# Batch 0's v read on SyncE's queue, and the block sums of v of the later batches on GpSimd, in an attention kernel with an FFN behind it

## The chip, the cores and the metric

The kernel runs on one core of a Trainium2 chip. The metric is the device time of one execution in microseconds (us); a kernel is run several times, and its median counts. A profiled execution also has a span: the time from the first to the last instruction that the trace holds.

## What is computed

Four batches, eight heads, 768 positions, 64 numbers per head. Each query sees its neighbours within 15 positions, and beside them one summary key and value for every block of 32 positions: the maximum of the block's keys and the mean of its values. The result goes through an FFN with a gate that is cut at 0 and 6.

```python
k_sum = k.reshape(B, H, nb, block, D).max(axis=3)
v_sum = v.reshape(B, H, nb, block, D).mean(axis=3)
mask_l = np.abs(pos[:, None] - pos[None, :]) < window        # window = 16
scores_s = scale * einsum(q, k_sum) + log(block)             # block = 32
a = softmax(concat([where(mask_l, scores_l, -1e9), scores_s]))
x = a @ concat([v, v_sum])          # heads side by side: 3072 x 512
h = x @ w_in                        # 512 x 2048
out = (h * clip(h + 3, 0, 6) / 6) @ w_out
```

Inputs and output are f32; the kernel multiplies in bf16.

## The kernel before, in words

The heads are taken in four pairs (p = 0 to 3; two pairs make a group g), each batch in two halves of 384 queries. A pair's keys lie in kbd and its values in vbd, both block diagonal in 128 rows: the first head in rows 0 to 63, the second in 64 to 127, zeros elsewhere. For each batch and pair:

- K (L277) transposes k on PE into a PSUM tile tp, copies it into kbd (one half by ACT, one by DVE, L302) and takes the block maxima (red, L306, and kst, L313).
- Tq (L319) transposes q in the same way; ACT writes qT (L333). In batch 0 the queries come in two parts, up to 480 and from 480 on.
- Sl (L336) makes the scores of the near keys (PE L341), ACT their exp (L344), DVE multiplies by the mask (L345). Ss (L347) makes those of the blocks (PE L351, exp on ACT L354).
- AV (L368) accumulates num (the block sums in vst first, L377, then vbd, L379) and den, ACT makes 1/den with a logarithm and an exp (lg, L395 and L396), and DVE writes x (L397).

The FFN of a half is F1 (L402; 16 steps ft, each four matmuls L409, ACT's r L412 and DVE's g L413) and F2 (L415; 48 matmuls L422, copied out by ACT L426 and stored through SyncE's queue).

Values come in three ways. For batch 0, load_vf (L123) reads v as f32 into vf, two transfers of 64 x 12 x 64 per pair. vcast (L244) copies it into vbd, one half by ACT and one by DVE. vsum0 (L251) sums it on PE with an f32 matmul (vps, L256): for each group ACT and DVE copy the sums out (L261), SyncE's queue moves them into 96 rows (vs, L263), and to_vst (L228) multiplies them by the head masks hm4 into vst. For batches 1 to 3, load_v (L115) reads v into vbd, cast to bf16 by the transfer, and load_vrows (L132) reads it once more into vr, 96 rows of 4 x 512 f32, one per block; vsum (L233) sums a row on DVE with six additions (L235, L236, L237, and three of L240), and to_vst follows with two products (L230).

What sets the order: until `start.__exit__` (L474), PE, ACT and DVE run in the order in which the code is written, and GpSimd does so in the whole program. v_first (L442) is vcast, zeroing of vbd for pairs 0 and 1, and vsum0; it is written for pair 0 and pair 1 ahead of K(0, 0), for pairs 2 and 3 near S_first(0). After L474 a table `plan` lists for each slot (one step ft of the FFN's work list L532, 16 slots per entry) which pieces of attention are issued there, and a scheduler may move them by some steps; `attention` (L489) fills it.

All loads are issued by GpSimd (POOL), one after another, and wait on POOL for their buffers. Each also waits for the load eight places ahead of it. Before the FFN the order is v of pairs 0 and 1, k and q of pair 0, v of pair 2, the mask, v of pair 3, k and q of pair 1, of pairs 2 and 3 together, hm4, then w_in in four chunks (one ahead of the others, L214), the second part of q, and w_out in four. `hold_loads` (L517) is a copy on POOL that reads a column of g of F1(0, 11), so that the loads of batch 1 are issued only after it. In batches 1 to 3, load_vrows(b + 1, g) stands in POOL's order right after vsum(b, g), and shares two buffers with it.

Of the kernel before, what the change touches and what calls it, by code (L numbers as in the profile page):

```python
# [32 lines left out]
def kernel(  # L33
# [50 lines left out]
    def load_k(b, p, n=1):  # L84

        if b < NLONG:
            t = ld.tile([RP, 2 * n, RUN, D], BF16, tag=f"kb{n}", name="kb", bufs=2)
            nc.gpsimd.dma_start(out=t[:], in_=k[b, 2 * p:2 * p + 2 * n].rearrange("h (p s) d -> p h s d", s=RUN))
        else:
            t = ld.tile([128, NT, 2, D], BF16, tag="kb", name="kb")  # L90
            load_natural(t, k, b, p)
        for i in range(n):
            kb_t[b, p + i] = t, i
# [29 lines left out]
    def load_vf(p):  # L123

        if not vf:
            t = gp.tile([128, NP, NK, D], F32, tag="g", name="vf")
            vf.update({i: t[:, i] for i in range(NP)})
        for j in range(2):
            nc.gpsimd.dma_start(out=vf[p][64 * j:64 * j + 64],  # L129
                                in_=v[0, 2 * p + j].rearrange("(n k) d -> k n d", k=KB))  # L130

    def load_vrows(b, g):  # L132
# [9 lines left out]
    def load_w_in(c):  # L142
        w = d_ff // 4
        nc.gpsimd.dma_start(out=w_in_sb[:, :, c * w:(c + 1) * w], in_=w_in_v[:, :, c * w:(c + 1) * w])

    def load_w_out(c):
# [4 lines left out]
    ctx.enter_context(tc.manual_schedule(engines={ET.Pool}))  # L151
    start = tc.manual_schedule(engines={ET.PE, ET.Activation, ET.DVE})
    start.__enter__()
    load_vf(0)
    ident = const.tile([128, 128], BF16, tag="id", name="ident")
    nc.gpsimd.memset(ident[:], 1.0)
    nc.gpsimd.affine_select(out=ident[:], in_=ident[:], compare_op=ALU.is_equal, fill=0.0, base=0,
                            channel_multiplier=1, pattern=[[-1, 128]])
    load_vf(1)
    load_k(0, 0)  # L160
    load_q(0, 0, 1, 0)
    load_vf(2)


    mask = const.tile([128, WIN], BF16, tag="mask", name="mask")
    nc.gpsimd.memset(mask[:], 1.0)
    for j in range(2):
# [2 lines left out]
                                channel_multiplier=-1, pattern=[[1, WIN]])  # L170
        nc.gpsimd.affine_select(out=m, in_=m, compare_op=ALU.is_ge, fill=0.0, base=2 * HALO,
                                channel_multiplier=1, pattern=[[-1, WIN]])
    load_vf(3)
    load_k(0, 1)
    load_q(0, 1, 1, 0)
    load_k(0, 2, 2)
    load_q(0, 2, 2, 0)


    hm4 = const.tile([RS, 4, D], F32, tag="hm4", name="hm4")  # L180
# [27 lines left out]
            nc.vector.memset(ind[32 * i:32 * i + 32, par, par, i:i + 1], 1.0)  # L208
    for p in range(NP):
        zero_off_diagonal(nc.vector if p < 2 else nc.scalar, kbd[p][:])  # L210
    for p in range(2, NP):
        zero_off_diagonal(nc.vector, vbd[p])
    NK0 = 7
    load_w_in(0)  # L214

    def zero_rest():
        for p in range(NP):
# [7 lines left out]
        nc.vector.memset(half_c[:], 0.5)  # L225


    def to_vst(g, a):  # L228
        for par in range(2):
            nc.vector.tensor_tensor(vst[2 * g + par][:], a.unsqueeze(1).to_broadcast([RS, 2, D]), hmv[par],  # L230
                                    op=ALU.mult)

    def vsum(b, g):  # L233
        r, w = vr_t[b, g], BLK // PCS * D
        nc.vector.tensor_tensor(r[:, 0:1, 0:w], r[:, 0:1, 0:w], r[:, 2:3, 0:w], op=ALU.add)  # L235
        nc.vector.tensor_tensor(r[:, 1:2, 0:w], r[:, 1:2, 0:w], r[:, 3:4, 0:w], op=ALU.add)  # L236
        nc.vector.tensor_tensor(r[:, 0, 0:w], r[:, 0, 0:w], r[:, 1, 0:w], op=ALU.add)  # L237
        while w > D:
            w //= 2
            nc.vector.tensor_tensor(r[:, 0, 0:w], r[:, 0, 0:w], r[:, 0, w:2 * w], op=ALU.add)  # L240
        to_vst(g, r[:, 0, 0:D])


    def vcast(p):  # L244
# [32 lines left out]
    def K(b, p):  # L277

        red = work.tile([128, NB], BF16, tag="red", name="red")
        if b >= NPE:  # L280
            t = kT[b, p]
            for j in range(2):
                rows = slice(64 * j, 64 * j + 64)
                nc.vector.tensor_copy(kbd[p][rows, :, rows], t[rows].rearrange("p (n c) -> p n c", c=KB))
            nc.vector.reduce_max(red[:], t[:].rearrange("p (n c) -> p n c", c=BLK), axis=AX.X)
        else:
            pool, tag = (ps_o, "o") if b == 0 else (ps_s, "s")
            tp = pool.tile([128, S], BF16, tag=tag, name="tp")
            (t, i), long = kb_t[b, p], b < NLONG
            if long:  # L290
                for s in range(RUN):
                    for j in range(2):
                        nc.tensor.transpose(tp[64 * j:64 * j + 64, s * RP:(s + 1) * RP], t[:, 2 * i + j, s], ident[0:RP, 0:RP])
            else:
                for s in range(NT):
                    nc.tensor.transpose(tp[:, s * 128:(s + 1) * 128], t[:, s].rearrange("p h d -> p (h d)"), ident[:])
            for j in range(2):
                copy = nc.scalar.copy if j == 0 or (b == 1 and p % 2 == 1) else nc.vector.tensor_copy
                rows = slice(64 * j, 64 * j + 64)
                o = kbd[p][rows, :, rows]  # L300
                if long:
                    copy(o.rearrange("p n (c s) -> p n c s", s=RUN), tp[rows].rearrange("p (s n c) -> p n c s", s=RUN, n=NK))  # L302
                else:
                    copy(o, tp[rows].rearrange("p (n c) -> p n c", c=KB))
            if long:
                nc.vector.tensor_reduce(red[:], tp[:].rearrange("p (s n c) -> p n s c", s=RUN, n=NB), axis=AX.XY, op=ALU.max)  # L306
            else:
                nc.vector.reduce_max(red[:], tp[:].rearrange("p (n c) -> p n c", c=BLK), axis=AX.X)
        off = 2 * NB * (p % 2)
        o = kst[p][:, off:off + 2 * NB].rearrange("p (h n) -> p h n", h=2)  # L310
        if b == 0:
            for i in range(2):
                nc.vector.tensor_tensor(  # L313
                    o[:, :, i * NK:(i + 1) * NK], red[:].rearrange("p (n i) -> p i n", i=2)[:, i:i + 1].to_broadcast([128, 2, NK]),
                    hmk[:, :, 0:NK], op=ALU.mult)
        else:
            nc.vector.tensor_tensor(o, red[:].unsqueeze(1).to_broadcast([128, 2, NB]), hmk[:], op=ALU.mult)
# [50 lines left out]
    def AV(b, p, half):  # L368
# [1 line left out]
        if s not in xt:  # L370
            xt[s] = xp.tile([128, NP, HALF], BF16, tag="x", name="x")
        a, asm = at[p], asum[b, p // 2, half]
        alt = b == 0 and (p == 3 or p == 1 and half == 1)
        pool = ps_o if alt else ps_n
        num = pool.tile([128, HALF], F32, tag="o" if alt else "num", name="num")
        bl = blocks_of(half)
# [51 lines left out]
            nc.sync.dma_start(out=out[row:row + 128], in_=o[:])  # L428


    load_w_in(1)
    load_q(0, 0, 4, 1)
    for c in range(2, 4):
# [6 lines left out]
            Sl(0, p, lo, hi)  # L440

    def v_first(p):  # L442
        vcast(p)
        if p < 2:
            zero_off_diagonal(nc.scalar, vbd[p])
        vsum0(p)

    v_first(0)
    zero_rest()
    v_first(1)  # L450
    K(0, 0)
    Tq(0, 0, 0)
    v_first(2)
    S_first(0)
    v_first(3)
    K(0, 1)
    Tq(0, 1, 0)
    S_first(1)
    nc.vector.tensor_scalar_mul(osum4[:], hm4[:], float(BLK))
    to_vst(0, vs96[0][:])  # L460
    K(0, 2)
    Tq(0, 2, 0)
    Ss(0, 0, 0)
    AV(0, 0, 0)
    K(0, 3)
    Tq(0, 3, 0)
    S_first(2)
    AV(0, 1, 0)
    to_vst(1, vs96[1][:])
    S_first(3)  # L470
    Ss(0, 1, 0)
    AV(0, 2, 0)
    AV(0, 3, 0)
# [5 lines left out]
    def at_slot(s, f):  # L479
        plan.setdefault(int(s), []).append((s, f))  # L480
# [5 lines left out]
            at_slot(2 * p + 3, lambda g=p // 2: Ss(0, g, 1))  # L486
        at_slot(12 + p, lambda p=p: AV(0, p, 1))

    def attention(b, t_slot, t_gap, av_slot, av_gap, loads):  # L489
        for p in range(NP):  # L490
            s = t_slot + t_gap * p
            if b < NPE:
                at_slot(s + 1, lambda p=p: Tq(b, p))
            else:
                at_slot(s - 3, lambda p=p: X(b, p))
            at_slot(s, lambda p=p: K(b, p))
            s += 4
            at_slot(s, lambda p=p: Sl(b, p, 0, 4))
            at_slot(s + 0.5, lambda p=p: Sl(b, p, 4, 8))
            at_slot(s + 1, lambda p=p: Sl(b, p, 8, 12))  # L500
            if p % 2 == 1:
                at_slot(s + 2, lambda g=p // 2: Ss(b, g, 0))
                at_slot(s + 3, lambda g=p // 2: Ss(b, g, 1))
                at_slot(s, lambda g=p // 2: vsum(b, g))
                if b + 1 < B:
                    at_slot(s, lambda g=p // 2: load_vrows(b + 1, g))
            if 2 <= b + 1 < B:
                at_slot(s + 1, lambda p=p: (load_k(b + 1, p), load_q(b + 1, p)))
        for i, (p, half) in enumerate(((0, 0), (1, 0), (2, 0), (3, 0), (0, 1), (1, 1), (2, 1), (3, 1))):
            at_slot(av_slot(i), lambda p=p, half=half: AV(b, p, half))  # L510
            if half == 1 and b + 1 < B:
                if p % 2 == 1:
                    at_slot(av_slot(i), lambda g=p // 2: load_v(b + 1, g))

    pace = const.tile([1, 2], BF16, tag="pace", name="pace")

    def hold_loads(t, ft):  # L517

        nc.gpsimd.tensor_copy(pace[:], gt[t][0:1, ft, 0:2])

    at_slot(11, lambda: hold_loads(0, 11))
    for g in range(2):
        at_slot(11.5, lambda g=g: (load_k(1, 2 * g, 2), load_q(1, 2 * g, 2)))
        at_slot(15, lambda g=g: load_v(1, g))
        at_slot(15, lambda g=g: load_vrows(1, g))
    attention(1, 28, 3, lambda i: (41, 42, 45, 46, 50, 52, 54, 56)[i], 2, None)
    for b in range(2, B):
        base = 48 + 32 * (b - 2)
        order = (14, 16, 24, 26, 18, 20, 28, 30)
        attention(b, base, 5, lambda i, base=base: base + order[i], 2, None)  # L530

    work_list = ([(0, None), (1, 0), (None, 1), (2, None)] + [(t, t - 1) for t in range(3, NTILE)]  # L532
                 + [(None, NTILE - 1)])
# [40 lines left out]
```

## Time and profile before

| | |
|---|---|
| median of 6 runs | 262.68 us (260.35 to 263.92) |
| the profiled execution: time, span | 261.92 us, 260.2 us |
| PE busy | 239.8 us (92%) |
| DVE busy | 157.0 us (60%) |
| ACT busy | 167.7 us (64%) |
| POOL busy | 71.7 us (28%), 104 instructions |
| POOL's queue of transfers | 19.14 MB in 53264 packets |
| SyncE's queue of transfers | 6.34 MB in 3664 packets |
| vf loads (L129, POOL) | 8 of 192 KB, 3.9 us from issue to landing |
| vr loads (L136, POOL) | 6 of 768 KB, 7.8 us |

A group line of the profile names the code line, engine, operation, what it writes and reads, and how often; then busy time and the mean of one. In brackets stands how long the engine was idle before it and who ended that. PEld is PE's weight load, SP is SyncE, and a q behind an engine is its sequencer, which issues transfers. A PE that counts as busy is not PE at its full rate: matmuls overlap, and their ends are modelled. In a line of the timeline the first number is the start, the second the time until the last of the merged instructions ended.

### The profile page before, as it was taken

What the parts mean: (1) busy time and instruction counts of PE and PEld (TensorE: products, weight loads), DVE (VectorE), ACT (ScalarE), POOL (GpSimd) and SP (SyncE); (2) the same over time, 40 slices, a digit from 0 to 9 for tenths busy, and PEclk for the clock granted to TensorE, in tenths of its full rate; (3) what the DMA queues carried; (4) which work ended last, traced back from release to release, by engine and by line L of the source; (5) the groups of instructions that cost most, each with busy time, mean ns of one, the idle gap of its engine ahead of it and who ended that gap; (6) DMA issues with size and microseconds to landing.
All of it is one profiled execution on the core that took longest, in us unless ns stands there. A gap on an engine that the chain in (4) does not pass through costs nothing.

```text
span 260.2 us, 4992 instructions
## 1 busy us (share of the span) xinstructions
PE 239.8 (92%) x1936; PEld 135.8 (52%) x1936; DVE 157.0 (60%) x362; ACT 167.7 (64%) x325; POOL 71.7 (28%) x104
## 2 busy tenths in 40 slices
PE   0957889999999979999999999999999999999993
PEld 0225546644455546666645555566655555555541
DVE  6396656624899667998894477657544444444400
ACT  7565679833787858998666656766856655555410
POOL 8993000847281402796710400000000000000000
PEclk9996899999999999999999999999999999999999
DMA  3999995699999912999991551101011111101122
GB/s 111 181 151 199 206 207 91 93 190 230 219 241 98 184 45 49 87 162 154 195 108 40 35 69 42 43 1 43 0 40 43 40 40 43 40 2 42 41 81 81
DMA packets 56951, 25.80 MB, mean 99 GB/s; under 512 B 45152, under 2 KB 52320, under 8 KB 56928
## 3 DMA queue, kind: packets, MB, share of 16 engines
q0 software_dynamic: 53264, 19.14, 64.4%
q1 hardware_dynamic: 3664, 6.34, 6.5%
q8 instruction: 15, 0.25, 0.4%
q14 instruction: 8, 0.07, 0.1%
HBM read 31.98 MB, written 6.29 MB: 147 GB/s over the span
## 4 chain that ended last, share of the span: by engine, by line
PE 60%; DMA 15%; DVE 11%; POOL 7%; ACT 4%; issue 3%; POOLq 0%; ACTq 0%
PE hp L409 24%; PE op L422 23%; DMA vr<-in_v_dram 10%; DVE g L413 3%; DMA qb<-in_q_dram 3%; PE num L379 2%; POOL vf L129 2%; POOL vbd L120 2%; DMA kb<-in_k_dram 2%; PE num L377 2%; PE den L383 2%; PE den L386 2%; PE sl L341 2%; PE ss L351 1%; ACT r L412 1%
## 5 line engine op out<-in xcount | busy, mean ns | idle before, releaser
L409 PE MATMUL hp<-x,win 128*128 128x384 bf16 x512 | 104.5, 326 | 2.8 <-DVE g L413 1.5
L412 ACT ACTIVATE r<-hp,half_c 128x384 f32<-128x384 f32 x128 | 73.5, 580 | 45.6 <-PE hp L409 44.8
L422 PE MATMUL op<-wout,g 128*128 128x512 bf16 x384 | 101.0, 379 | 0.0
L413 DVE SCALAR_TENSOR_TENSOR g<-r,hp 128x384 bf16<-128x384 f32 x128 | 69.8, 552 | 46.1 <-ACT r L412 46.0
L409 PEld LDWEIGHTS <-win 128*128 128x128 bf16 x512 | 47.4, 98 | 36.9 <-issue 6.0
L422 PEld LDWEIGHTS <-g 128*128 128x128 bf16 x384 | 36.6, 98 | 32.5 <-issue 0.6
L397 DVE TENSOR_TENSOR x<-num,lg 128x384 bf16<-128x384 f32 x32 | 17.8, 555 | 25.1 <-ACT lg L396 23.8
L120 POOL DMA_DIRECT2D vbd<-in_v_dram x24 | 18.1, 776 | 36.5 <-PE num L379 33.3
L395 ACT ACTIVATE lg<-den 128x384 f32<-128x384 f32 x32 | 15.7, 491 | 17.8 <-PE den L390 9.2
L344 ACT ACTIVATE at<-sl 128x376 bf16<-128x376 f32 (+2 forms) x48 | 22.3, 486 | 3.7 <-PE sl L341 3.6
L426 ACT COPY ot<-op 128x512 f32<-128x512 f32 x24 | 13.8, 583 | 8.9 <-PE op L422 8.8
L345 DVE TENSOR_TENSOR at<-at,mask 128x376 bf16<-128x376 bf16 (+2 forms) x48 | 16.2, 350 | 3.6 <-ACT at L344 3.5
L396 ACT ACTIVATE lg<-lg 128x384 f32<-128x384 f32 x32 | 16.8, 525 | 0.8
L379 PEld LDWEIGHTS <-vbd 128*128 128x128 bf16 x224 | 13.2, 101 | 7.9 <-issue 4.5
L341 PE MATMUL sl<-qT,kbd 128*128 128x94 bf16 x192 | 14.6, 209 | 2.2 <-DVE kbd L302 2.1
L341 PEld LDWEIGHTS <-kbd 128*128 128x128 bf16 x192 | 12.0, 99 | 8.9 <-DVE kbd L302 3.0
L113 POOL DMA_DIRECT2D qb<-in_q_dram x16 | 13.5, 865 | 4.7 <-DMA vr<-in_v_dram 2.7
L379 PE MATMUL num<-at,vbd 128*128 128x94 bf16 (+2 forms) x224 | 14.4, 204 | 0.0
L256 PE MATMUL vps<-vf,ind 128*8 128x384 f32 x16 | 8.2, 662 | 6.4 <-DMA vf<-in_v_dram 6.4
L113 POOL DMA_DIRECT2D kb<-in_k_dram x16 | 13.5, 866 | 0.0
L377 PE MATMUL num<-asum,vst 96*128 96x384 bf16 x32 | 10.8, 337 | 2.3 <-DVE x L397 1.5
L386 PE MATMUL den<-at,obd 128*128 128x384 bf16 x32 | 11.1, 345 | 0.0
(82 smaller groups left out, 218.3 us busy)
## 6 DMA issues: line engine op xcount, KB each, us to landing
out_dram<-ot SPq DMA_DIRECT2D x24, 256.0 KB, 2.1
vr<-in_v_dram POOLq DMA_DIRECT2D x6, 768.0 KB, 7.8
vbd<-in_v_dram POOLq DMA_DIRECT2D x24, 96.0 KB, 4.2
win<-in_moe_w_in_dram POOLq DMA_DIRECT2D x4, 512.0 KB, 12.0
wout<-in_moe_w_out_dram POOLq DMA_DIRECT2D x4, 512.0 KB, 18.9
vf<-in_v_dram POOLq DMA_DIRECT2D x8, 192.0 KB, 3.9
kb<-in_k_dram POOLq DMA_DIRECT2D x16, 96.0 KB, 6.8
qb<-in_q_dram POOLq DMA_DIRECT2D x16, 96.0 KB, 6.4
```

Source lines behind the costliest of these rows:

```text
L113: nc.gpsimd.dma_start(out=t[:, :, j], in_=src[b, 2 * p + j].rearrange("(s p) d -> p s d", p=128))
L120: nc.gpsimd.dma_start(out=vall[rows, p, lo:hi, rows], in_=v[b, 2 * p + j].rearrange("(n k) d -> k n d", k=KB)[:, lo:hi])
L341: nc.tensor.matmul(sp[:, i * WIN:(i + 1) * WIN], kbd[p][:, t], qT[p][:, PAD - HALO + t * KB:PAD - HALO + t * KB + WIN], start=True, stop=True)
L344: nc.scalar.activation(a, sp[:, 0:n * WIN].rearrange("p (n c) -> p n c", c=WIN), AF.Exp, scale=scl)
L379: nc.tensor.matmul(num[:, lo:hi], vbd[p][:, t], a[:, t, off:off + hi - lo], start=False, stop=(i == len(bl) - 1))
L386: nc.tensor.matmul(d3, ones, a[:, t0:t1, HALO:HALO + KB], start=False, stop=False)
L396: nc.scalar.activation(lg[:], lg[:], AF.Exp, scale=-1.0)
L397: nc.vector.tensor_tensor(xt[s][:, p], num[:], lg[:], op=ALU.mult)
L409: nc.tensor.matmul(hp[:], w_in_sb[:, kt, ft * 128:(ft + 1) * 128], xt[t][:, kt], start=(kt == 0), stop=(kt == NP - 1))
L412: nc.scalar.activation(r[:], hp[:], AF.Relu, bias=half_c[:], scale=1.0 / 6.0)
L413: nc.vector.scalar_tensor_tensor(gt[t][:, ft], r[:], 1.0, hp[:], op0=ALU.min, op1=ALU.mult)
L422: nc.tensor.matmul(op[:], gt[t][:, ft, ts * 128:(ts + 1) * 128], w_out_sb[:, ft], start=(ft == 0), stop=(ft == NFT - 1))
```

## The change

Three things. First, load_vf issues on SyncE, and all eight of its transfers come first; on POOL k and q of all pairs now come before the mask and hm4. Second, the first chunk of w_in is held by a copy on POOL that reads a column of vf of pair 3, so it is issued when that has landed. Third, the six additions and two products of vsum run on GpSimd, and the slots of vsum and load_vrows are set anew.

With it go edits of the order in batch 0: vsum0 comes ahead of vcast; v_first(p) stands after Tq(0, 0), S_first(0), K(0, 2) and Ss(0, 0, 0); vbd is zeroed for pairs 0 and 1 on ACT at the start and for pairs 2 and 3 on DVE after v_first(0); AV(0, 0, 0) comes after S_first(2). K's tp of batch 0 is taken from ps_h, where Tq's is, and num and den of batch 0 come from ps_o for more pairs.

```diff
         for j in range(2):
-            nc.gpsimd.dma_start(out=vf[p][64 * j:64 * j + 64],
+            nc.sync.dma_start(out=vf[p][64 * j:64 * j + 64],
...
-    load_vf(0)
+    for p in range(NP):
+        load_vf(p)
+    load_k(0, 0)
+    load_q(0, 0, 1, 0)
     ident = const.tile([128, 128], BF16, tag="id", name="ident")
...
-    load_vf(1)
-    load_k(0, 0)
-    load_q(0, 0, 1, 0)
-    load_vf(2)
+    load_k(0, 1)
+    load_q(0, 1, 1, 0)
+    load_k(0, 2, 2)
+    load_q(0, 2, 2, 0)
...
+    pace = const.tile([128, 2], F32, tag="pace", name="pace")
+    def hold_loads(src):
+        nc.gpsimd.tensor_copy(pace[0:src.shape[0], 0:1], src)
...
-    for p in range(2, NP):
-        zero_off_diagonal(nc.vector, vbd[p])
+    for p in range(2):
+        zero_off_diagonal(nc.scalar, vbd[p])
     NK0 = 7
-    load_w_in(0)
...
-    def to_vst(g, a):
+    def to_vst(eng, g, a):
...
-        nc.vector.tensor_tensor(r[:, 0:1, 0:w], r[:, 0:1, 0:w], r[:, 2:3, 0:w], op=ALU.add)
+        nc.gpsimd.tensor_tensor(r[:, 0:1, 0:w], r[:, 0:1, 0:w], r[:, 2:3, 0:w], op=ALU.add)
...
-        to_vst(g, r[:, 0, 0:D])
+        to_vst(nc.gpsimd, g, r[:, 0, 0:D])
...
-            pool, tag = (ps_o, "o") if b == 0 else (ps_s, "s")
+            pool, tag = (ps_h, "h") if b == 0 else (ps_s, "s")
...
-        alt = b == 0 and (p == 3 or p == 1 and half == 1)
+        alt = b == 0 and (half == 0 and p != 2 or half == 1 and p % 2 == 1)
...
+    hold_loads(vf[NP - 1][:, 0, 0:1])
+    load_w_in(0)
     load_w_in(1)
...
     def v_first(p):
+        vsum0(p)
         vcast(p)
-        if p < 2:
-            zero_off_diagonal(nc.scalar, vbd[p])
-        vsum0(p)
-    v_first(0)
     zero_rest()
-    v_first(1)
     K(0, 0)
     Tq(0, 0, 0)
-    v_first(2)
+    v_first(0)
+    for p in range(2, NP):
+        zero_off_diagonal(nc.vector, vbd[p])
     S_first(0)
-    v_first(3)
+    v_first(1)
     K(0, 1)
...
     K(0, 2)
+    v_first(2)
     Tq(0, 2, 0)
     Ss(0, 0, 0)
-    AV(0, 0, 0)
+    v_first(3)
     K(0, 3)
     Tq(0, 3, 0)
     S_first(2)
+    AV(0, 0, 0)
+    S_first(3)
+    to_vst(nc.vector, 1, vs96[1][:])
     AV(0, 1, 0)
...
-                at_slot(s, lambda g=p // 2: vsum(b, g))
-                if b + 1 < B:
-                    at_slot(s, lambda g=p // 2: load_vrows(b + 1, g))
...
+        for g in range(2):
+            at_slot(sums[g], lambda g=g: vsum(b, g))
+            if b + 1 < B:
+                at_slot(rows, lambda g=g: load_vrows(b + 1, g))
...
-    attention(1, 28, 3, lambda i: (41, 42, 45, 46, 50, 52, 54, 56)[i], 2, None)
+    attention(1, 28, 3, lambda i: (41, 42, 45, 46, 50, 52, 54, 56)[i], (30, 31), 45)
...
-        attention(b, base, 5, lambda i, base=base: base + order[i], 2, None)
+        attention(b, base, 5, lambda i, base=base: base + order[i], (base + 4.5, base + 8.5) if b == 2 else (base - 11.5, base - 1.5), base + 12)
```

In POOL's order the two sums of batch 1 now stand between the loads of vr of batch 1 and the k and q loads of batch 2. Each sum of batches 2 and 3 stands right after the vbd loads of its group; the vr loads of a batch stand behind k and q loads.

More of the change, by code (lines that the diff above doesn't have):

```diff
@@ L172 @@
                                 channel_multiplier=1, pattern=[[-1, WIN]])
[L173 to L177, printed above, removed]
+    pace = const.tile([128, 2], F32, tag="pace", name="pace")
+    def hold_loads(src):
+        nc.gpsimd.tensor_copy(pace[0:src.shape[0], 0:1], src)
     hm4 = const.tile([RS, 4, D], F32, tag="hm4", name="hm4")
@@ L225, in zero_rest @@
         nc.vector.memset(half_c[:], 0.5)
-    def to_vst(g, a):
+    def to_vst(eng, g, a):
         for par in range(2):
-            nc.vector.tensor_tensor(vst[2 * g + par][:], a.unsqueeze(1).to_broadcast([RS, 2, D]), hmv[par],
+            eng.tensor_tensor(vst[2 * g + par][:], a.unsqueeze(1).to_broadcast([RS, 2, D]), hmv[par],
                                     op=ALU.mult)
@@ L234, in vsum @@
         r, w = vr_t[b, g], BLK // PCS * D
-        nc.vector.tensor_tensor(r[:, 0:1, 0:w], r[:, 0:1, 0:w], r[:, 2:3, 0:w], op=ALU.add)
-        nc.vector.tensor_tensor(r[:, 1:2, 0:w], r[:, 1:2, 0:w], r[:, 3:4, 0:w], op=ALU.add)
-        nc.vector.tensor_tensor(r[:, 0, 0:w], r[:, 0, 0:w], r[:, 1, 0:w], op=ALU.add)
+        nc.gpsimd.tensor_tensor(r[:, 0:1, 0:w], r[:, 0:1, 0:w], r[:, 2:3, 0:w], op=ALU.add)
+        nc.gpsimd.tensor_tensor(r[:, 1:2, 0:w], r[:, 1:2, 0:w], r[:, 3:4, 0:w], op=ALU.add)
+        nc.gpsimd.tensor_tensor(r[:, 0, 0:w], r[:, 0, 0:w], r[:, 1, 0:w], op=ALU.add)
         while w > D:
             w //= 2
-            nc.vector.tensor_tensor(r[:, 0, 0:w], r[:, 0, 0:w], r[:, 0, w:2 * w], op=ALU.add)
-        to_vst(g, r[:, 0, 0:D])
+            nc.gpsimd.tensor_tensor(r[:, 0, 0:w], r[:, 0, 0:w], r[:, 0, w:2 * w], op=ALU.add)
+        to_vst(nc.gpsimd, g, r[:, 0, 0:D])
     def vcast(p):
@@ L459 @@
     nc.vector.tensor_scalar_mul(osum4[:], hm4[:], float(BLK))
-    to_vst(0, vs96[0][:])
+    to_vst(nc.vector, 0, vs96[0][:])
     K(0, 2)
+    v_first(2)
     Tq(0, 2, 0)
     Ss(0, 0, 0)
-    AV(0, 0, 0)
+    v_first(3)
     K(0, 3)
@@ L467 @@
     S_first(2)
+    AV(0, 0, 0)
+    S_first(3)
+    to_vst(nc.vector, 1, vs96[1][:])
     AV(0, 1, 0)
-    to_vst(1, vs96[1][:])
-    S_first(3)
     Ss(0, 1, 0)
@@ L487, with attention @@
         at_slot(12 + p, lambda p=p: AV(0, p, 1))
-    def attention(b, t_slot, t_gap, av_slot, av_gap, loads):
+    def attention(b, t_slot, t_gap, av_slot, sums, rows):
         for p in range(NP):
@@ L513, in attention @@
                     at_slot(av_slot(i), lambda g=p // 2: load_v(b + 1, g))
[L515 to L521, printed above, removed]
+    at_slot(11, lambda: hold_loads(gt[0][0:1, 11, 0:1]))
     for g in range(2):
```

## The prediction

> **What bounds the kernel now.** I read the busy time by stage first, then the first 36 us in order of time, then the waits and the instructions around the longest PE gap in the middle. Columns of the stage view: stretch, its length, then busy time and number of instructions of PE, PEld, DVE, ACT, POOL, the granted clock, the DMA share and GB/s.
>
> ```profile
> 0.00:35.00 35.00, 22.71 (x236) 11.62 (x237) 22.53 (x76) 22.08 (x42) 20.44 (x37) 0.90 0.98 173
> 35.00:55.00 20.00, 19.67 (x208) 11.84 (x206) 12.08 (x24) 16.22 (x35) 7.29 (x11) 1.00 0.81 131
> 55.00:137.00 82.00, 78.36 (x707) 45.87 (x706) 64.82 (x149) 59.88 (x118) 41.02 (x52) 1.00 1.43 148
> 137.00:260.00 123.00, 119.06 (x793) 66.48 (x790) 57.57 (x114) 69.57 (x132) 3.00 (x4) 1.00 0.15 40
> ```
>
> From 137 us on PE is full, and nothing that the change touches is there: no gain. Until 35 us no engine is full: PE is busy 22.7 of 35. From 55 to 137 PE is nearly full, DVE at 79%. Gaps between the starts of successive matmuls, less the matmul's own columns at full clock, sum to 7.9 us between 50 and 140 us, and under 1 us after it.
>
> The start, in order of time:
>
> ```profile
> 9.69 1.50 POOL L129 DMA_DIRECT2D vf<-in_v_dram  x2
> 11.17 0.66 POOL L88 DMA_DIRECT2D kb<-in_k_dram  x1
> ...
> 12.05 6.61 SPq L263 DMA_DIRECT2D vs<-vs  x2
> ...
> 14.58 1.45 PE L256 MATMUL vps<-vf,ind 128*8 128x384 f32 x4 [0.31 <-DMA vf<-in_v_dram]
> ...
> 19.92 0.53 PE L293 MATMUL tp<-ident,kb 96*64 96x96 bf16 x16 [0.53 <-DMA kb<-in_k_dram]
> ...
> 21.25 0.44 PE L332 MATMUL tp<-ident,qb 60*64 60x60 bf16 x16 [0.80 <-DMA qb<-in_q_dram]
> ```
>
> POOL issues one load after another at 0.66 to 0.8 us each, v ahead of k and q, so the last k and q of batch 0 arrive at 19.9 and 21.2 us. x of the first half is complete at 34.5 us (the matmuls of L409 that read it start at 34.55), and the steady FFN begins there.
>
> The middle:
>
> ```profile
> DVE vr L235 <- DMA vr<-in_v_dram: 5.1, 4, 2.2
> ```
> ```profile
> 90.14 0.69 DVE L235 TENSOR_TENSOR vr<-vr 96x512 f32<-96x512 f32 x1 [2.18 <-DMA vr<-in_v_dram]
> ...
> 90.27 0.54 ACT L396 ACTIVATE lg<-lg 128x384 f32<-128x384 f32 x1
> ...
> 92.75 0.55 DVE L397 TENSOR_TENSOR x<-num,lg 128x384 bf16<-128x384 f32 x1
> ...
> 93.34 0.32 PE L377 MATMUL num<-asum,vst 96*128 96x384 bf16 x1 [1.52 <-DVE x L397]
> ```
>
> DVE stands still for vr's transfer, then does its sums ahead of L397. lg was ready at 90.8, x came at 92.75: the longest PE gap of the middle.
>
> **What the Trainium skill says.** "DMA: Bandwidth & Descriptors", Queues, rings and completion order: each DMA engine takes turns between queues, packet by packet. The trace agrees in part: SyncE's 256-byte vs packets went out at one per 90 ns and engine (first transfer) and 240 ns (second) while GpSimd's queue was full. "SBUF — State Buffer", Who interferes with whom: a DVE instruction with two SBUF inputs and a GpSimd instruction that reads SBUF lock each other out. No run here shows it yet. "TensorE: Matmul & The Clock Gate", What's actually happening: PE runs at half clock until it has been busy for some 3.4 us. Here f32 matmuls of 384 columns took 0.66 us before 11.5 us and 0.365 after it, and the records show half clock again from 21.7 to 28.6 us.
>
> **The change at the start.** Removed from POOL ahead of k and q: eight vf issues of 0.794 us. POOL now starts k(0,0) at 1.33 and, with 0.67 us per issue and 0.65 for ident between, ends its six k and q issues at about 6. A first k took 4.1 us to land, so k(0,0) is in at about 5.4 (its transposes: 11.31 before), q(0,0) at 6.2. The six transfers are 78 packets of 1024 B per DMA engine; at 90 ns each with SyncE's turns between, the last lands at about 11 (before: 21.2).
>
> Added on SP: eight issues. SP has nothing else ahead of them; queued behind them are the two vs transfers, first due at about 14. An issue there took 0.33 us (out) to 0.83 (vs); at 0.8, all are out by 7.5. The unknown is how fast 6144 packets of 256 B, 384 per DMA engine, drain. Nearest rows: 256-byte packets of SyncE's queue took 18 to 31 ns each (SBUF to SBUF), casts of 256 read bytes 32. Lower bound 17 ns, upper bound 120; below nothing is excluded, bytes must move. I take 20 to 25: 75 packets go before GpSimd's queue fills at 3.7, 31 to 78 while it is full, the rest after 11. So pair 0's v (96 packets) is in at 6 to 11, pair 1's (192) at about 13, pair 3's at about 17 (before 14.5). v is later, k and q earlier.
>
> PE's order now puts pair 0's vps before Sl(0), pair 1's vps before K(0,1), so the start hangs on pair 1's v. From 13: two cold vps matmuls 1.3; ACT vs copy 0.47, vcast 0.83, kbd copy 0.79, to about 15.9 after its queue; then DVE's list. kbd 0.96, red 0.96, kst 0.28, masks 0.6, osum 0.43, vst 0.48 = 3.7; kbd, red, kst of pair 2, 2.2; vcast, vs, vcast 1.75; pair 3's kbd, red, kst 2.2; masks, x, masks, vst 2.25; three more x 1.7: sum 13.8, to 29.7, plus 0.8 for turns in which ACT is behind: x complete at 30.5 instead of 34.5, **4.0 us** gained.
>
> Edits at nothing: vbd's zeroing on DVE (1.87 us) and ACT lies before pair 1's v is in; gone that cover, up to 1.9. K's tp in ps_h waits for the previous red, which ends about when PE gets there (0.2). num and den in ps_o are as serial as in ps_n. The mask is made by 8, needed at 11. The hold: w_in(0) goes out at about 17.5 (15.1 before), into an empty queue; 512 KB per chunk at the 200 GB/s of the DMA row is 2.6 us, so the chunks land at about 22, 25, 28 and 31, with q's second part between, and F1 needs them at 30.5 and every 2.8 us after that (4 of 0.7). Each us that v is later than 25 costs one there. wout (4 more) is in by 42, F2 starts at 46. The vs transfer of pairs 2 and 3 now meets w_in: 5.5 us as its second did before (17.96 to 23.4); out at 22, vst at 28, as in the list.
>
> **The change in the middle.** The view of the instructions that touch vr (durations are least, median, most):
>
> ```profile
> L240 DVE TENSOR_TENSOR vr<-vr x18: 214/282/421, 68.3 to 135.6; 96x256 f32<-96x256 f32 x6, 96x128 f32<-96x128 f32 x6, 96x64 f32<-96x64 f32 x6
> L230 DVE TENSOR_TENSOR vst<-vr,hm x12: 279/282/288, 69.3 to 147.7; 96x128 bf16<-96x128 f32 x12
> ...
> L235 DVE TENSOR_TENSOR vr<-vr x6: 680/687/689, 63.5 to 130.4; 96x512 f32<-96x512 f32 x6
> ```
>
> Removed from DVE, six times: 3 of 0.68 (L235 to L237), then 0.41, 0.28, 0.21 (L240), and two of 0.28 (L230) = 3.5 us, 21 in all, and 5.1 us of waiting for vr. What PE gets back, gap by gap: 93.35 (1.68) ends with x, which could have come 1.9 earlier: 1.6. 123.7 (0.80), behind L235 at 120.99 and kbd: 0.7. 133.7 and 135.4 (0.94), between vr sums: 0.8. 65.3, 68.3, 73.6 (0.96): 0.7. The many small ones: 0.4. Sum 4.2.
>
> Added on POOL, six times the same. POOL's trace has no such operation; the skill's "GPSIMD Engine Reference", Elementwise — side-by-side cycle accounting, gives 4497 ns for 2048 f32, 2.2 ns per element: 512 are 1.1 us, 1.2 with 0.1 of its own. Three of 1.2, then 0.66, 0.38, 0.24, two of 0.38: 5.6 us per sum, 34 in all. Lower bound DVE's 3.5, upper twice 5.6. Behind them in POOL's queue stand the k and q loads of the next batch. vr(1,0) lands at about 59.5 (63.5 less 4), vr(1,1) at 64: the sums run to 71. Then 16 loads of 0.82, 13.1: 71 to 84; k(2,0) is in by 75, needed at 93 (L296, near 97 before); pair 3's in by 88, needed at 108. Batch 2's sums wait for AV(1,1,1), near 98 now, and four vbd issues of 0.76: 102 to 108, vst needed at about 113 (118.6 before). Slack 5 us; at 11 us per sum it is gone. Later sums have more. Against it stand DVE's masks (0.35 us, 12 per batch, two SBUF inputs): if half a dozen per batch meet a 1.2-us sum for 0.6, DVE loses 3.6 of the 7 it gained, PE some 0.7. Net **3.5 us**. DVE at 53% instead of 79% can hide that.
>
> **The sum.** Span 260.2 less 4.0 less 3.5 = 252.7; around it 1.72 (261.92 for that execution), so 254.4. The median of the runs is 0.76 over that execution: 255.2.
>
> **Rivals.** *v too slow to help*: at 35 to 40 ns per packet pair 1's v comes at 15, pair 3's at 22; from pair 3's vps to the end are 11.2 us (vps 1.3, then 9.9 as from K(0,3), 24.65, to 34.55), so x at 33 to 34: only the middle gains, 259. For it: SyncE's 240 ns per packet beside a full queue. Against: the 18 ns. *The sums on POOL give nothing*: the port lock, or sums of 11 us that make vst late; then 258.7. For it: POOL is in order, and a late sum holds every load behind it; against: the slack above. *Slower*: SyncE's queue drains v at 80 ns per packet or more. Pair 3's v is in at 3 + 384 x 0.08 = 33.7, x at 45, 10.5 later than before, less 3.5: 269.7. It decides from 62 ns on: v at 26.8 plus 11.2 is 38, which eats the 3.5. For it: one transfer of 96 pieces took SP 0.83 us to issue, and if that grows with the pieces (768), the last issue ends near 50. Against: 128 pieces took 0.33. *Better than thought*: v at 17 ns, pair 1's at 9: 251.
>
> **How the numbers follow.** Likeliest 0.52 (its own range 252 to 258.5); v no help 0.18; sums no help 0.10; slower 0.13; better 0.07. The range 250.5 to 262.5 leaves out the slower case and half of the better one. Within 1% (260.05 to 265.3, about what this measurement can tell from no change) lie the weak ends of the second and third, 0.14; slower 0.13; faster 0.73.
>
> **What would show it.** Right: first L293 near 5.5; K(0,1) right after pair 1's vps near 13 to 15; last x of the first half near 30.5; POOL sums of 5 to 6 us; no PE gap before L377 near 90. Wrong: long waits of vps for vf, w_in after 25, vst waited for by L377, masks of over 1 us.

## The result and the profile after

The changed kernel takes 265.12 us (median of 29 runs, 261.69 to 267.17), the kernel before beside it 263.18 (66 runs, 260.35 to 266.32); the ratio is 1.0043, 95% interval 1.0019 to 1.0067. The ratio leaves out, on both sides, executions more than 1.5% above the fastest of their kernel (ten of the changed kernel's), and so lies below the quotient of the medians. The kernel is slower by 0.4%, where 255.2 was forecast. The profiled execution took 265.47 us with a span of 263.6 (before: 261.92 and 260.2).

The stage view of the kernel after, with the columns of the one shown of before, and below it one stretch by itself, in the kernel after and in the one before:

```profile
0.00:35.00 35.00, 20.64 (x257) 10.91 (x258) 23.14 (x79) 23.67 (x45) 14.30 (x30) 1.00 1.01 164
35.00:55.00 20.00, 20.00 (x194) 11.76 (x193) 11.39 (x23) 14.98 (x32) 7.94 (x12) 1.00 0.99 160
55.00:137.00 82.00, 75.47 (x679) 44.71 (x677) 54.82 (x99) 57.79 (x114) 61.34 (x79) 0.96 1.13 132
137.00:263.50 126.50, 122.46 (x811) 68.41 (x809) 58.59 (x114) 71.59 (x136) 19.11 (x25) 1.00 0.25 48
```
```profile
105.00:125.00 20.00, 14.13 (x109) 9.10 (x108) 17.82 (x29) 11.12 (x24) 19.22 (x26) 0.83 0.67 43
```
```profile
105.00:125.00 20.00, 19.12 (x185) 12.56 (x182) 19.09 (x45) 17.16 (x37) 17.49 (x23) 1.00 1.83 137
```

The work did leave DVE: 54.8 us instead of 64.8 between 55 and 137 us. Yet PE is busy less than before there (75.5 of 82, not 78.4), and almost all of what it lacks lies in 105 to 125 us: 14.1 busy of 20, at a granted clock of 0.83. To date the loss I compared both traces (after less before). X of the first half complete: -1.8 us. Then the last matmul of each step of F1. Step 34 to 40, up to 105 us: -3.6. Step 42: +1.2. Step 48, at 124 us: +5.4. Step 60 to the end: +3.4. So the change was 3.6 us ahead at 105 us, lost 8.9 in the next 19, and won 2 back. All this is one execution: of the 29, seven took 261.7 to 262.8 us and the others 264.0 to 267.2, and no trace of the quicker kind was kept.

In what follows SBUF and PSUM are the two memories in which the kernel's tiles lie: what PE writes (tp, sl, num, hp) is in PSUM; at, mask, red, hmk, kst, r, vr, vst and x are in SBUF. The place in the timeline of the kernel after, GpSimd and DVE in order of time:

```profile
101.96 1.50 POOL L120 DMA_DIRECT2D vbd<-in_v_dram  x2 [1.74 <-PE num L382]
...
102.58 3.61 DVE L348 TENSOR_TENSOR at<-at,mask 128x376 bf16<-128x376 bf16 x1
103.45 1.30 POOL L238 TENSOR_TENSOR vr<-vr 96x512 f32<-96x512 f32 x1
104.69 1.28 POOL L239 TENSOR_TENSOR vr<-vr 96x512 f32<-96x512 f32 x1
106.05 1.27 POOL L240 TENSOR_TENSOR vr<-vr 96x512 f32<-96x512 f32 x1
```

A mask (L348, L345 before) that takes 0.35 us elsewhere takes 3.61: it begins while GpSimd issues loads, and ends at 106.20, after the second addition of the first of batch 2's two sums (105.97). Five more masks of batch 2 took 0.95, 1.30, 1.42, 1.26 and 0.65; the excess of the six is 7.1 us. The rows of the mask in the kernel before and in the one after (least, median, most):

```profile
L345 DVE TENSOR_TENSOR at<-at,mask x48: 296/348/405, 15.9 to 185.7; 128x376 bf16<-128x376 bf16 x40, 128x282 bf16<-128x282 bf16 x4, 128x470 bf16<-128x470 bf16 x4
```
```profile
L348 DVE TENSOR_TENSOR at<-at,mask x48: 301/354/3614, 12.5 to 189.1; 128x376 bf16<-128x376 bf16 x40, 128x282 bf16<-128x282 bf16 x4, 128x470 bf16<-128x470 bf16 x4
```

The same rows of two other instructions of DVE, in the kernel before (kst alone) and in the one after:

```profile
L317 DVE TENSOR_TENSOR kst<-red,hmk x12: 175/177/183, 68.2 to 179.3; 128x48 bf16<-128x48 bf16 x12
```
```profile
L320 DVE TENSOR_TENSOR kst<-red,hmk x12: 176/178/674, 65.8 to 182.7; 128x48 bf16<-128x48 bf16 x12
L416 DVE SCALAR_TENSOR_TENSOR g<-r,hp x128: 536/554/556, 33.8 to 249.2; 128x384 bf16<-128x384 f32 x128
```

kst reads two operands in SBUF, as the mask does, and is stretched too (0.67, 0.57 and 0.38 us instead of 0.18, each beside GpSimd's sums). g reads one in SBUF and one in PSUM; 25 of its 128 ran beside GpSimd's sums, and none took over 0.56 us.

DVE works in order, so kbd, red, kst, g and x behind a held mask are late as well, and PE stands (timeline of PE, kernel after; in brackets the idle time and who ended it):

```profile
110.15 0.48 PE L380 MATMUL num<-asum,vst 96*128 96x384 bf16 x1 [3.66 <-DVE x L400]
...
119.41 0.53 PE L354 MATMUL ss<-qT,kst 128*96 128x384 bf16 x2 [2.14 <-DVE red L311]
```

The first of these matmuls takes 0.48 us instead of 0.33: after each gap PE ran at half clock for some 3.5 us (109.9 to 113.3, 120.1 to 123.6). Half of these 6.9 us, some 3.4 us of PE's work, comes on top of its idle time, so 7.1 us of DVE became more than that on PE.

The start: k was transposed first at 5.89 us, pair 1's vps began at 11.33, x of the first half was complete at 32.7 (before 34.5). The last of the gain went here (timeline of DVE, kernel after):

```profile
18.39 0.49 DVE L233 TENSOR_TENSOR vst<-vs,hm 96x128 bf16<-96x128 f32 x2 [1.33 <-DMA vs<-vs]
...
28.75 0.49 DVE L233 TENSOR_TENSOR vst<-vs,hm 96x128 bf16<-96x128 f32 x2 [1.88 <-DMA vs<-vs]
```

### The profile page after: what moved, and what is told of

The parts are those of the page before. It is cut to its first block, busy times and chain, and to the rows that moved or that the text cites. A ratio compares the mean times of both kernels' runs of the same rounds, so it can differ in the third digit from the quotient of the medians.

```text
span 263.6 us, 5002 instructions
## 1 busy us (share of the span) xinstructions
PE 238.6 (91%) x1936; PEld 135.8 (52%) x1936; DVE 147.9 (56%) x314; ACT 168.0 (64%) x325; POOL 102.7 (39%) x145
## 4 chain that ended last, share of the span: by engine, by line
PE 69%; DVE 11%; DMA 9%; ACT 6%; SPq 2%; issue 2%; ACTq 0%
PE op L425 28%; PE hp L412 26%; DMA vf<-in_v_dram 4%; DVE at L348 3%; DMA out_dram<-ot 3%; DVE g L416 3%; PE num L382 3%; DMA vs<-vs 2%; PE sl L344 2%; SPq L129 2%; PE num L380 2%; PE ss L354 2%; PE den L386 2%; PE den L389 1%; DVE red L311 1%
## 5 line engine op out<-in xcount | busy, mean ns | idle before, releaser
L412 PE MATMUL hp<-x,win 128*128 128x384 bf16 x512 | 105.8, 329 | 1.1 <-DVE g L416 0.4
L416 DVE SCALAR_TENSOR_TENSOR g<-r,hp 128x384 bf16<-128x384 f32 x128 | 69.8, 552 | 54.8 <-ACT r L415 53.6
L348 DVE TENSOR_TENSOR at<-at,mask 128x376 bf16<-128x376 bf16 (+2 forms) x48 | 23.6, 500 | 7.5 <-ACT at L347 7.4
L386 PE MATMUL den<-asum,osum 96*128 96x384 bf16 x32 | 10.5, 330 | 1.3 <-DVE x L400 1.3
```

What stands on the lines that cost most here:

```text
L348: nc.vector.tensor_tensor(a, a, mask[:].unsqueeze(1).to_broadcast([128, n, WIN]), op=ALU.mult)
L412: nc.tensor.matmul(hp[:], w_in_sb[:, kt, ft * 128:(ft + 1) * 128], xt[t][:, kt], start=(kt == 0), stop=(kt == NP - 1))
L416: nc.vector.scalar_tensor_tensor(gt[t][:, ft], r[:], 1.0, hp[:], op0=ALU.min, op1=ALU.mult)
```

## The experiments

My theory after this: the sums on GpSimd take from the masks a path into SBUF that both need, and the start gains little since batch 0's own block sums come late. The main rival: the new start delivers something late, or leaves an order behind, that costs the 9 us. Twelve kernels in three sets, each set on one chip with the kernel before (262.53, 262.68 and 262.82 us). A ratio is always to the kernel before of its own set; differences between kernels of two sets are taken from the ratios.

**The two halves apart.** Start only: vsum back on DVE in the slots of before. Sums only: the start of before.

```diff
-    def vsum(b, g):
+    def vsum(b, g, eng=nc.gpsimd):
...
+                at_slot(s, lambda g=p // 2: vsum(b, g, nc.vector))
+                if b + 1 < B:
+                    at_slot(s, lambda g=p // 2: load_vrows(b + 1, g))
...
```

> The start of the changed kernel alone: v of batch 0 on SyncE's queue, w_in held; all block sums on DVE at the slots of the kernel before, each followed by the load of the next vr. Theory (the masks of batch 2 lose the SBUF port to the sums on GpSimd): x of the first half is complete about 1.8 us before that of the kernel before, and this stays to the end: about 1.8 us faster, some 261.4 beside 263.2; every mask of L348's kind takes 0.34 to 0.41 us. Rival (what the new start delivers late, or the order it leaves behind, costs the 9 us between 105 and 124 us): the loss appears here too, time at or above the kernel before.

> The start of the kernel before, all six sums of batches 1 to 3 on GpSimd at the slots of the changed kernel. Theory (port lost in batch 2): the masks of batch 2 are stretched by some 7 us in sum as in the changed kernel, and without the 1.8 us of the start the time is about 267, 3.8 over the kernel before. Rival (the start causes the loss): about 261, since only the 1.8 us won before 105 us are left.

Start only: 262.26, ratio 1.000 (0.997 to 1.003); no mask over 0.41. Sums only: 265.44, ratio 1.012 (1.008 to 1.016); four masks of batch 2 are stretched by 5.2 us in sum, and PE stands 3.6 us before L377:

```profile
112.60 0.32 PE L377 MATMUL num<-asum,vst 96*128 96x384 bf16 x1 [3.64 <-DVE x L397]
```

The loss belongs to the sums, and needs no new start: the main rival falls. The start was worth less than the 1.8 of one trace: in its profiled execution x of the first half was complete 0.6 us earlier than before, in the median nothing is left. The halves do not add up: the sums alone cost 1.2%, with the new start 0.4%. Why they cost less behind it is not shown.

**Batch 2's sums taken away from the masks**, once to DVE (in the slots of before), once to an earlier time on GpSimd, with the loads of its vr ahead of the loads of k and q. This is the edit of the second:

```diff
-        to_vst(nc.gpsimd, g, r[:, 0, 0:D])
+        if b != 2:
+            vprod(b, g)
+    def vprod(b, g):
+        to_vst(nc.gpsimd, g, vr_t[b, g][:, 0, 0:D])
...
+            if b == 2:
+                at_slot(base + (4.5, 8.5)[g], lambda g=g: vprod(b, g))
...
-    attention(1, 28, 3, lambda i: (41, 42, 45, 46, 50, 52, 54, 56)[i], (30, 31), 45)
+    attention(1, 28, 3, lambda i: (41, 42, 45, 46, 50, 52, 54, 56)[i], (30, 31), 32)
...
-        attention(b, base, 5, lambda i, base=base: base + order[i], (base + 4.5, base + 8.5) if b == 2 else (base - 11.5, base - 1.5), base + 12)
+        attention(b, base, 5, lambda i, base=base: base + order[i], (43.2, 44.2) if b == 2 else (base - 11.5, base - 1.5), base + 12)
```

> The changed kernel with the two sums of batch 2 back on DVE at the slots of the kernel before; those of batches 1 and 3 stay on GpSimd. Theory (port lost in batch 2 alone): no mask over 0.41 us, the gaps of PE at 110 and 119 us are gone; DVE gets 7 us of sums back, PE pays some 1.5 of it: about 259, 6 below the changed kernel and 4 below the one before. Rival (any sums on GpSimd cost about what they free, wherever they stand): 262 to 265, a third of the loss gone.

> The changed kernel with the vr loads of batch 2 issued ahead of the k and q loads of batch 2, its twelve additions on GpSimd right after these (some 90 to 101 us, where DVE has no masks), and only the four products left at their place. Theory: masks of batch 2 free of stretching but for 0.5 us at the products, nothing goes back to DVE: 257 to 259, 7 below the changed kernel. Rival (GpSimd is late with what stands behind the sums, so vst or the k, q and v loads come late): no better than the changed kernel, since the additions now stand ahead of the v loads of batch 2 as well, 2.5 us later than before.

The first came out at 269.0 (ratio 1.026, 1.021 to 1.030), against both theories, and for a reason of its own. Line of DVE:

```profile
97.21 0.69 DVE L238 TENSOR_TENSOR vr<-vr 96x512 f32<-96x512 f32 x1 [8.03 <-DMA vr<-in_v_dram]
```

The scheduler put the sum ahead of masks and x in DVE's order, while vr's loads now stand behind 16 loads of k and q: DVE waited 8.0 us, PE 8.1. No mask was stretched (0.39 us at most). It says only that the sum and the load that feeds it must move together.

The second: 259.59, ratio 0.989 (0.985 to 0.993). The row of its masks:

```profile
L352 DVE TENSOR_TENSOR at<-at,mask x48: 301/354/550, 12.3 to 182.7; 128x376 bf16<-128x376 bf16 x40, 128x282 bf16<-128x282 bf16 x4, 128x470 bf16<-128x470 bf16 x4
```

The same additions on the same engine, begun at 94.1 us instead of 103.5, and the most a mask takes falls from 3.61 to 0.55. The time is 1.5%, some 3.9 us, below the changed kernel.

**Is it the two operands in SBUF?** In the changed kernel, with nothing moved, the mask is added to the scores in PSUM ahead of the exp (0 or -30000), so that DVE's instruction has one operand in SBUF:

```diff
...
-        nc.scalar.activation(a, sp[:, 0:n * WIN].rearrange("p (n c) -> p n c", c=WIN), AF.Exp, scale=scl)
-        nc.vector.tensor_tensor(a, a, mask[:].unsqueeze(1).to_broadcast([128, n, WIN]), op=ALU.mult)
+        s3 = sp[:, 0:n * WIN].rearrange("p (n c) -> p n c", c=WIN)
+        nc.vector.tensor_tensor(s3, s3, mask[:].unsqueeze(1).to_broadcast([128, n, WIN]), op=ALU.add)
+        nc.scalar.activation(a, s3, AF.Exp, scale=scl)
```

> The changed kernel with one edit in every piece of near scores, in all batches: the mask is added to the scores in PSUM (0 or -30000) ahead of the exp, instead of multiplied to its result in SBUF. DVE's instruction then has one operand in SBUF and one in PSUM; nothing else is changed, the sums of batch 2 stand where they stood. Theory (two operands in SBUF against GpSimd's reads of SBUF): every mask takes the same time, 0.5 to 0.6 us for f32 from PSUM, beside the sums of batch 2 too, and the gaps of PE at 110 and 119 us are gone: 259 to 262, although DVE pays about 0.2 us for each of 44 masks. Rival (GpSimd's sums slow whatever DVE does meanwhile, or the transfers do): masks of over 1 us remain between 102 and 123 us, time at or above the changed kernel.

```profile
L348 DVE TENSOR_TENSOR sl<-sl,mask x48: 446/550/655, 12.4 to 187.6; 128x376 f32<-128x376 f32 x40, 128x282 f32<-128x282 f32 x4, 128x470 f32<-128x470 f32 x4
```
```profile
L320 DVE TENSOR_TENSOR kst<-red,hmk x12: 171/181/860, 70.8 to 181.3; 128x48 bf16<-128x48 bf16 x12
```
```profile
121.19 1.01 DVE L348 TENSOR_TENSOR sl<-sl,mask 128x376 f32<-128x376 f32 x2
121.41 1.35 POOL L238 TENSOR_TENSOR vr<-vr 96x512 f32<-96x512 f32 x1
...
122.64 1.33 POOL L239 TENSOR_TENSOR vr<-vr 96x512 f32<-96x512 f32 x1
123.05 0.56 DVE L348 TENSOR_TENSOR sl<-sl,mask 128x376 f32<-128x376 f32 x1 [0.27 <-PE sl L344]
```

Three masks beside the additions shown, 0.55 each, as everywhere (the 0.45 and 0.66 of the row are the smaller and larger pieces); of this size, twelve in the whole kernel ran beside GpSimd's sums, at 0.54 to 0.56. The gaps at 110 and 119 are gone. kst, left with its two operands in SBUF, is stretched here as well, up to 0.86 us. So it is the pair of operands, not GpSimd's work as such nor the transfers. The time is 264.71 (1.006, 1.004 to 1.009), not the 259 to 262 expected: the dearer mask, now ahead of the exp, puts x of the first half at 37.0 us instead of 32.7 already (ACT waits 14.2 us for masks in all).

**What holds the path while GpSimd issues loads?** The masks at 113.51 and 114.73 of the changed kernel took 1.30 and 1.42 us beside four issues of vbd, when no addition had begun by the trace:

```profile
113.25 3.04 POOL L120 DMA_DIRECT2D vbd<-in_v_dram  x4
113.51 2.64 DVE L348 TENSOR_TENSOR at<-at,mask 128x376 bf16<-128x376 bf16 x2
...
116.23 1.35 POOL L238 TENSOR_TENSOR vr<-vr 96x512 f32<-96x512 f32 x1
```

The edit puts two tiny instructions ahead of each of batch 2's sums, a memset of columns that nothing else uses and a copy of one of them:

```diff
+        if b == 2:
+            nc.gpsimd.memset(r[:, 0:1, w:w + 8], 0.0)
+            nc.gpsimd.tensor_copy(r[:, 2:3, w:w + 1], r[:, 0:1, w:w + 1])
```

> The changed kernel, and on GpSimd two tiny instructions ahead of each of batch 2's two sums: a memset of 8 unused columns of vr, and a copy of one of them, which has to wait for the memset on all of GpSimd's processors. Theory (in the changed kernel the processors [...]start the sum while GpSimd still issues the loads of v, and hold the port): the masks that overlapped only load issues (1.30 and 1.42 us, at 113.5 and 114.7; the head of the 3.61-us one, before 103.4) fall to 0.35; those beside additions stay long; some 2 us of 7 are saved, 264 or a little less. Rival (the issue of loads itself holds the port): these masks stay over 1 us, time 265.1 or more.

```profile
114.94 3.04 POOL L120 DMA_DIRECT2D vbd<-in_v_dram  x4
...
116.12 0.35 DVE L351 TENSOR_TENSOR at<-at,mask 128x376 bf16<-128x376 bf16 x1
116.95 0.35 DVE L351 TENSOR_TENSOR at<-at,mask 128x376 bf16<-128x376 bf16 x1 [0.49 <-ACT at L350]
...
118.30 1.26 POOL L241 TENSOR_TENSOR vr<-vr 96x512 f32<-96x512 f32 x1
118.31 1.47 DVE L351 TENSOR_TENSOR at<-at,mask 128x376 bf16<-128x376 bf16 x1
```

The masks beside issues are free, the one that meets an addition (118.30 to 119.56) is not: as the theory said, and the issue itself holds nothing. The gain is larger than I had put it: 260.66 (ratio 0.992, 0.988 to 0.996), 1.2% or some 3.2 us below the changed kernel, with 1.4 us of excess left in batch 2. Since DVE gets on by 105 us, its later masks also meet fewer additions. That GpSimd's other processors begin the addition ahead fits the Trainium skill ("GPSIMD Engine Reference", Instruction dispatch: a core goes on to the next instruction as soon as its own share is done); the trace does not show single processors, so this much stays an inference. The memset and the copy together take it away; which of the two does it was not tried.

**The start.** On the kernel with the early additions (259.59): vs copied by ACT and put on ACT's queue; the weights after w_in's first chunk held until the second vs has landed; and both.

```diff
-                (nc.vector.tensor_copy if h else nc.scalar.copy)(a[:, h * (NK // 2):(h + 1) * (NK // 2)], vps[g, h][:])
+                nc.scalar.copy(a[:, h * (NK // 2):(h + 1) * (NK // 2)], vps[g, h][:])
...
-            nc.sync.dma_start(out=vs96[g][:], in_=a[:])
+            nc.scalar.dma_start(out=vs96[g][:], in_=a[:])
...
     v_first(3)
+    hold_loads(vs96[1][:, 0:1])
+    load_w_in(1)
...
```

> The kernel with batch 2's additions early (259.6 us), and in its start both halves of vps copied by ACT and the vs transfers put on ACT's own queue instead of SyncE's. Theory (the start gained little because the block sums of batch 0 come late twice: vs of pairs 0 and 1 stands behind vf in SyncE's queue, 4 us, and this delays DVE's copy for pairs 2 and 3): DVE's wait before the first vst is gone (0.4 to 1.7 us), the second vs is issued near 20.8 instead of 22.7, lands as many us earlier, x of the first half is complete 1.5 to 2 us earlier: about 257.8. Rival (the start is bound by the serial work of PE, ACT and DVE, vs is not what ends last): x within 0.5 us, 259 to 260.

> The kernel with batch 2's additions early, and in its start only the first chunk of w_in behind the hold on vf; all that follows it on GpSimd's queue is issued once the second vs has landed. Theory (the 6 us of the second vs transfer are the weights' traffic): it lands 2 to 3 us after its issue, near 25.5 instead of 28.7, AV of pair 2 no longer waits for it: x of the first half about 1.5 us earlier, 258; w_in's second chunk is issued near 25.5 and lands before 31. Rival (the 6 us are the transfer's own): still 28.7, and w_in is then issued near 29, so F1 waits for it: 2 to 4 us slower, 262 to 264.

> Both edits of the start together, on the kernel with batch 2's additions early: vs copied by ACT and moved on ACT's queue, the weights from the second chunk on held until it has landed. Theory: vs of pairs 2 and 3 is issued near 20.8 and in by 23, DVE never waits for it, x of the first half complete near 30 instead of 32.5 to 34: about 256. Rival (serial work binds): no further gain over the better of the two, about 258 to 260.

ACT's queue: 263.26 (1.002, 0.998 to 1.005), and with both 263.52 (1.000, 0.997 to 1.003): worse by 1.2% than the kernel that it was made from, and by 1.9% than with held weights alone, against either theory. ACT works in order too. Its second copy, the wait for PE and the issue of vs (1.27 us from 14.85 on) stand ahead of its half of kbd of pair 1, and DVE's half waits for that (with ACT's queue alone):

```profile
17.72 0.96 DVE L309 COPY kbd<-tp 64x768 bf16<-64x768 bf16 x1 [3.83 <-ACT kbd L309]
```

Without the edit it began at 15.24 and had waited 0.16. PE stands 3.6 us instead of 1.5. The same happens at pair 3 (28.50 instead of 23.63, a wait of 3.64), and x of the first half is complete at 39.2 instead of 34.95. DVE did not wait for vs any more, as forecast, but nothing was won by it.

The held weights: 257.99 (0.981, 0.974 to 0.988). The second vs was in 2.5 us after its issue at 22.96, when the copy that waits for it could start:

```profile
25.43 0.17 POOL L181 COPY pace<-vs 96x1 f32<-96x1 f32 x1 [5.60 <-DMA vs<-vs]
```

In the kernels with the same start and free weights DVE had waited to 6.1 to 6.6 us after the issue: these 6 us were the weights' traffic. What that did to x is less sure. x of the first half was complete at 32.6 in the profiled execution, and at 32.3 and 33.0 in the two later ones with held weights; without, it came at 34.95 in the kernel this one was made from, but at 32.7 in the changed kernel, and at 33.9 to 34.2 in three others with its start. The interval also overlaps that of the kernel it was made from.

**Each part by itself again**, and the best kernel with its products on DVE:

```diff
-        to_vst(nc.gpsimd, g, vr_t[b, g][:, 0, 0:D])
+        to_vst(nc.vector if b == 2 else nc.gpsimd, g, vr_t[b, g][:, 0, 0:D])
```

> The start of the changed kernel alone, all block sums on DVE as in the kernel before (the run that gave no gain, 262.26), and the weights after the first chunk of w_in held until the second vs has landed. Theory (the second vs in the weights' traffic took the start's gain): x of the first half about 1.9 us earlier than in the kernel before and this stays to the end: 260.6 to 261. Rival (the 1.9 of the run with both edits is chance of one execution): within 0.5 us of the kernel before.

> The start of the kernel before, all sums on GpSimd, with batch 2's additions early as in the run of 259.6. Theory (without the port's loss the middle gains what was forecast, 3.5 us, whatever the start does): 259 to 259.5 beside 262.6. Rival (a part of that run's gain came from its start): above 260.5.

> The best so far (258.0: batch 2's additions early, weights held behind vs) with batch 2's four products into vst on DVE, 0.28 us each, instead of on GpSimd. Theory: the mask of 1.04 us beside the products falls to 0.35, DVE pays 1.1 us for the products and gets 0.7 back: 257.3 to 258. Rival (DVE has no room there, or waits for GpSimd's last addition): 258.5 or more.

The old start with early sums: 259.59 (0.988, 0.985 to 0.992), the same as with the new start. The middle is worth 3.2 us by itself, the new start as it was made nothing that these runs show. The start with held weights and DVE's sums: 263.18 (0.999, 0.997 to 1.002), no gain, although its profiled execution, 260.31, had x of the first half 1.5 us earlier and was 1.8 ahead at the end; its 22 runs lie between 260.3 and 266.1, those with early sums on GpSimd and the same start within 1.6 us. Why is open, and the granted clock does not tell: it was 0.977 to 0.994 in its runs above 264 us and 0.985 to 0.991 in those below 262. The products on DVE: 258.07 (0.984, 0.980 to 0.987), no better than 257.99: the mask beside them is free, but two that meet additions at 101 to 104 us are stretched by 1.1 us (one of them by 0.6 without this edit too), and the first two products, themselves with two operands in SBUF, take 1.0 us instead of 0.5.

The best kernels beat both: 258 us, 4.7 below the kernel before (ratios 0.981 and 0.984).

## Why the prediction was wrong

**The step that failed: the port lock.** I wrote "if half a dozen per batch meet a 1.2-us sum for 0.6, DVE loses 3.6 of the 7 it gained, PE some 0.7". Six masks it was, in batch 2 alone. But they were held for 1.2 us each in the mean, not 0.6, and the longest through two additions and the issues ahead of them; and PE paid not 0.7 but, in the profiled execution, most of 8.9 us. kst, with the same pair of operands, was not in the sum at all. The conversion was the worse half. "DVE at 53% instead of 79% can hide that" is a mean over 82 us. The same view of the kernel before, cut to the place where batch 2's first sum was going to stand:

```profile
108.50:118.50 10.00, 9.90 (x95) 6.52 (x94) 9.78 (x25) 9.21 (x21) 10.00 (x14) 1.00 1.68 160
```

DVE is busy 9.78 of 10 us there, and of what the change removes only two products into vst, 0.6 us, lie in it: what holds a mask there goes straight to PE. The kernel before shows this by itself. The rule from "SBUF — State Buffer", Who interferes with whom, which I had cited as not shown, is now shown by the mask in PSUM: the full-size mask took 0.34 to 3.61 us with two SBUF operands, and 0.54 to 0.56 with one. In the other direction the runs show little: an addition took at most 1.44 us instead of 1.26.

**The middle's 3.5 us: right, for the wrong kernel.** The additions of 512 took 1.26 to 1.44 us (1.2 said), the later ones 0.74, 0.45 and 0.34, the products 0.45: 6.5 to 6.8 per sum instead of 5.6. Nothing in the middle was late for it: there, vst was not waited for. The long gap before 93 us went, as said. With batch 2's additions away from the masks the gain is 3.2 us, close to the 3.5; as kst and single masks were still held, the agreement is partly luck.

**The start's 4.0 us: a chain not followed.** v drained as forecast (18 to 31 ns per packet; pair 1's v in at 11.1 instead of 13, pair 3's at 18.3 instead of 17), k and q came when said, and DVE's kbd of pair 1 began at 14.1 instead of 15.9 (the terms given for it add up to 16.4). So DVE's list began 1.8 us ahead of its time; x, due at 30.5, came 2.2 behind. I even had the second vst "at 28, as in the list", and it came at 28.75. But the list ends at 29.7 with "three more x", as if the matmuls of pairs 2 and 3 that read that vst were done: in the kernel before, 4.1 us lie between the end of vst (30.4) and x (34.5). So 28.75 sets x near 33, and 32.7 was measured. The wait of 1.33 us for the first vs, issued behind vf in SyncE's queue, was not in the list at all: SP's issues of vf took not 0.8 but up to 3.65 us, the last until 13.77. Over several runs not even the 1.8 us remained, and the granted clock gives a likely reason: the records of that execution show no stretch at half clock up to 35 us (before: 21.7 to 28.6), while those of the four other kernels with this start and the same masks show 6.8 to 10.4 us of it there. The start of the changed kernel was lucky in its trace.

**The edits at nothing** held: w_in was issued at 18.9 (17.5 said) and F1 did not wait for it.

**The rivals.** "The sums on POOL give nothing" had the mechanism, the port lock, at 258.7 and a chance of 0.10: that took all of the middle's gain and more. The slower case was looked for only in vf's drain, where it wasn't. "Masks of over 1 us" was named as the sign, and it came.

## What to carry to other kernels

Work of this kind that goes to GpSimd can take back from DVE what it frees, where DVE's instructions beside it read two operands in SBUF (0.35 us became up to 3.61 here; those with one were never stretched). Place it where DVE has few of them, and judge DVE's slack in that very stretch, not over the stage. If loads are issued right ahead of such work, try a memset and a copy that waits for it between them, which freed the masks beside the issues here. When something is moved early, follow the chain behind the last thing that still comes late, here vst to x, before the list of busy times is believed.

## What was not expected of the hardware

A mask beside load issues alone was held when an addition stood next in GpSimd's order (1.30 and 1.42 us), and free (0.35) when a memset and a copy that waits for it stood between. A transfer of 96 pieces issued by ACT cost ACT 1.27 and 0.70 us of its own time. The same transfer on SyncE's queue took 6.1 to 6.6 us beside the weights, up to the first instruction that waited for it, and 2.5 without them.
